# The output product by Strassen's form over pairs of token tiles, its weights' seven sides streamed from DRAM

## The chip, the cores and the metric

The kernel runs on one core of a Trainium2 chip. A core has TensorE (matrix products into PSUM), VectorE, ScalarE and GpSimd (elementwise work), and SyncE, whose queue issues most of the transfers here. The engines run their own instruction streams in order and wait for each other by semaphores. The time is device microseconds (us) of one execution; the times shown are the median of the runs and their range. Beside them stands one profiled execution, whose trace every view below comes from.

## The reference

Two stages in float32. The first is attention with root-mean-square norms on queries and keys: batch 8, 12 heads, 448 tokens, head size 64. The second is a gated feed-forward block on all 3584 tokens, model size 768, hidden size 1536. The weights come as float64.

```python
scores = scale * np.matmul(q_n, k_n.transpose(0, 1, 3, 2))
attn = softmax(scores)
x = np.matmul(attn, v).transpose(0, 2, 1, 3).reshape(B * S, H * D)
g = x @ w_gate
h = g * (1.0 / (1.0 + np.exp(-g))) * (x @ w_val)
out = h @ w_out
```

## The kernel before

**Stages.** The kernel proper is `fast`. Two batches make a block of 2 x 448 = 896 tokens; there are four blocks (NB). Attention for block 0 comes first. Then each block has an up phase (x by w_gate and w_val, giving the hidden rows `gt`, 128 partitions by 6 groups by 2 halves by 896 tokens, with the hidden features on the partitions) and a down phase (the hidden rows by w_out, giving the output rows). The attention of the next block, 12 head pairs, is woven into the down phase; the last block's down phase stands alone.

**The up phase** already uses a form of Strassen's algorithm (Winograd's, with seven products). `block(n)` (L946) calls `half_block(g, which)` (L955) for six groups and for gate and value. Each half block loads four quarters of the weight from the DRAM scratch `quarters` into a tile `ws` (L963, two buffers), and GpSimd makes three more sides out of them and changes a fourth (L969). TensorE does seven products of three matmuls each (L985), alternating between two PSUM banks, and VectorE adds the pieces up (L1001). The seven sides of x lie in `xs`; `sides` (L817, L833) makes the sums among them on VectorE, after the last head pairs of a block. SiLU is made of a tanh on ScalarE (L1035, L1088) and products on VectorE (L1040, L1095 for the gate; L1048, L1104 for the value, after which a group's hidden rows are done). The list `hidden` holds the last two of every group.

**The down phase before.** The 896 tokens are 7 tiles of 128. For each tile and each half of the 768 output columns, `out_rows` (L1116, L1120) multiplies 12 chunks of hidden features into one PSUM bank, in two parts of six matmuls. The weight `wo` lies in SBUF whole. The first part waits for groups 0 to 2 only, the second for 3 to 5. ScalarE copies the bank out (L1130) and issues the store (L1141), two transfers or one as the tile falls on the rows of the output.

**The weights.** They are float64. `convert` (L858) loads the raw words (SP), and ScalarE (L870, L874) and VectorE (L879, L882, L893, L897) make float32 of them. Twelve conversions make the quarters of w_gate and w_val, from staging places in `gt` and `wo` into a spare piece of `gt` or of `xs`, and from there they go to DRAM (L925). Six more make w_out, in place in `wo` (L934).

**The order of the work** is planned when the kernel is built. Every step is a piece of the class `Order`: an engine, an estimated duration, a due time `when`, what it comes after, and which buffers it takes. `run` (L417) sorts each engine's pieces by due time and takes, over and over, the piece that could start earliest by its model; a later piece is preferred to an earlier one if it could start more than 0.02 us sooner:

```python
                    if choice is None or at < choice[0] - 0.02:
                        choice = (at, piece)
```

The chosen order becomes the engines' instruction streams; on the chip each engine keeps to it and waits where its operands aren't there. `port=True` marks VectorE and GpSimd pieces that the planner never lets overlap. The due times of a block come from constants (L558), where UP, DOWN and BOTH are the planned lengths of an up phase, of a down phase alone and of one with attention:

```python
    UP, DOWN, BOTH = 14 * NG * PRODUCT, 111.0, 212.0
```

In attention (L584) the steps that the text speaks of are: the transposes of queries and keys on TensorE (L667), the scores (L705), the exponentials on ScalarE (L715), their sums on GpSimd (L721, L724), the weighted values on TensorE (L753), the reciprocal and the division on VectorE (L796, L806), and GpSimd's inverse root of the norm (L635) and its scaling (L647).

Of the kernel before, what the change touches and what calls it, by code (L numbers as in the profile page):

```python
# [9 lines left out]
F32 = mybir.dt.float32  # L10
# [3 lines left out]
ALU = mybir.AluOpType  # L14
# [346 lines left out]
class Order:  # L361
# [22 lines left out]
    def add(  # L384
        self, engine, us, when, emit, after=(), takes=(), uses=(), port=False, kb=0, group=None,
        mode=None, early=None,
    ):
        piece = dict(
            engine=engine, us=us, when=when, emit=emit, takes=takes, port=port, kb=kb,
            group=group, mode=mode, early=early,  # L390
            after=[a for a in after if a is not None], end=None, n=len(self.pieces),
        )
# [24 lines left out]
    def run(self, lookahead=400):  # L417
        left = {}
        for piece in sorted(self.pieces, key=lambda p: (p["when"], p["n"])):
            left.setdefault(piece["engine"], []).append(piece)  # L420
        while any(left.values()):
            best = None
            for engine, pieces in left.items():
                choice = None
                last = self.last.get(engine, dict(group=None))
                for piece in pieces[:lookahead]:
                    at = self.start(piece)
                    if at is None:
# [12 lines left out]
            at, piece = best  # L441
# [21 lines left out]
def fast(  # L463
# [30 lines left out]


    nc = tc.nc
    B, H, S, D = q.shape
# [12 lines left out]
    NK = NW // 2  # L510
    NG = NF // 2


# [43 lines left out]
    PRODUCT = 2.27  # L557
    UP, DOWN, BOTH = 14 * NG * PRODUCT, 111.0, 212.0  # L558

# [257 lines left out]
    def sides(n, c, when):  # L817
# [33 lines left out]
    flat_gt = gt.rearrange("p g f t -> p (g f t)")  # L851
    flat_wo = wo.rearrange("p f c -> p (f c)")
# [50 lines left out]
    def up_weights(i, when):  # L903
# [24 lines left out]

    def down_weights(f, when):

        rows = moe_w_out.rearrange("(f p) c -> p f c", p=P)[:, ts(f, 2), :]
        place = (5, 4, 5, 5, 2, 2)[f]
        weights["o", f] = convert(
            lambda raw: nc.sync.dma_start(raw.rearrange("p (f c) -> p f c", f=2), rows),  # L934
            flat_wo[:, ts(f, 2 * DM)],
            place, when, [staged.get(3 + f // 2)],
        )


# [6 lines left out]
    def block(n):  # L946
# [8 lines left out]
        def half_block(g, which):  # L955
# [159 lines left out]

        def out_rows(bank, i, half, part):  # L1116

            for g in range(part * NG // 2, (part + 1) * NG // 2):
                for f in range(2):
                    nc.tensor.matmul(  # L1120
                        banks[bank][:, 0:HALF],
                        gt[:, g, f, ts(i, P)],
                        wo[:, f * NG + g, ts(half, HALF)],
                        start=(g == 0 and f == 0),
                        stop=(g == NG - 1 and f == 1),
                    )

        def evacuate(bank, i, half):
            rows = take("rows", (n, i, half), [P, HALF])
            nc.scalar.copy(rows, banks[bank][:, 0:HALF])  # L1130

        def store(i, half):

            rows = tiles["rows", (n, i, half)]
            at = first = i * P
# [7 lines left out]

        groups = [(i, half) for i in range(2 * S // P) for half in range(2)]
        span = (BOTH if n < NB - 1 else DOWN) / (2 * len(groups))
        for k, (i, half) in enumerate(groups):
            bank = turn[0]
            turn[0] = 1 - bank
            for part in range(2):
                last = add(  # L1150
                    "PE", 3.93, start + UP + (2 * k + part) * span,
                    lambda bank=bank, i=i, half=half, part=part: out_rows(bank, i, half, part),
                    after=[*hidden[part * NG : (part + 1) * NG], last, bank_read[bank]]
                    + ([weights["o", f] for f in range(NG)] if n == 0 else []),
                    mode="full",
                )
            when = start + UP + (2 * k + 2) * span
            bank_read[bank] = add(
                "ACT", 0.48, when, lambda bank=bank, i=i, half=half: evacuate(bank, i, half),
                after=[last], takes=[("rows", (n, i, half))],  # L1160
            )
            add(
                "ACT", 0.15, when, lambda i=i, half=half: store(i, half),
                after=[bank_read[bank]], uses=[("rows", (n, i, half))], kb=192,
            )
        down_done[n] = last
# [18 lines left out]
    for i in range(2 * NG):  # L1185
        up_weights(i, 14.0 + 13.0 * i)
    for f in range(NF // 2):
        down_weights(f, 14.0 + 13.0 * 2 * NG + 14.0 * f)
    for m in range(EARLY):
# [73 lines left out]
```

## Time and profile before

| | |
|---|---|
| median of the runs (range) | 1667.47 us (1666.97 to 1668.51) |
| the profiled execution: its time, its span | 1668.56 us, 1666.7 us |
| TensorE busy, weight loads | 1625.9 us (98%), 808.4 us (49%) |
| VectorE, ScalarE, GpSimd busy | 670.6, 401.6, 681.9 us |
| first stretch: attention alone | 0 to 169.4 us |
| an up phase (block 1), the down phase after it | 566.7 to 761.5, 761.5 to 965.0 us |
| last block: up phase, down phase and tail | 1363.3 to 1552.7, 1552.7 to 1666.7 us |
| HBM read, written | 99.09 MB, 20.45 MB |

The span runs from the first to the last instruction that the trace holds; the execution's own time is somewhat longer. A group of instructions in the profile is one source line on one engine, with the tiles that it writes and reads. A float32 matmul leaves two records in it. Engines overlap, so busy times don't add up to the span; what counts is which engine ends each stretch and what it waited for. The phases overlap a little at their seams, since the planner draws attention's first pieces into the end of an up phase.

### The profile page before, as it was taken

The numbers are of one execution on the slowest core, as the hardware profiler recorded it, in microseconds if no ns is written. First come the engines' busy times: TensorE is split into PE (matmuls) and PEld (weight loads), VectorE is DVE, ScalarE is ACT, GpSimd is POOL, SyncE is SP. The second block draws the span as 40 slices with busy tenths as digits, with TensorE's granted clock in tenths as the row PEclk, the third lists the DMA queues.
The fourth block names the chain that finished last, engine by engine and source line by source line (L and its number), as shares of the span: only waits on it lengthen the run. The fifth ranks groups of instructions, "written<-read, shape, count | busy, mean of one in ns | idle before, by whom it ended". The sixth has DMA issues, their size and how long they took to land.

```text
span 1666.7 us, 14502 instructions
## 1 busy us (share of the span) xinstructions
PE 1625.9 (98%) x5616; PEld 808.4 (49%) x5616; DVE 670.6 (40%) x689; ACT 401.6 (24%) x537; POOL 681.9 (41%) x452
## 2 busy tenths in 40 slices
PE   5998999999999999999999999999999999999998
PEld 2333455545444455544545455554454545555555
DVE  5899763343334333333324333343323433333100
ACT  5765331123332110122333200102333211001000
POOL 5653223356675222445566502244567532221000
PEclk9999999999999999999999999999999999999999
DMA  8885531301111011221111111221211101111010
GB/s 234 250 235 184 183 146 64 96 28 48 54 43 67 11 57 57 66 71 44 48 48 42 58 42 39 68 76 37 64 48 49 63 15 57 38 57 39 15 29 25
DMA packets 73009, 120.57 MB, mean 72 GB/s; under 512 B 5860, under 2 KB 63716, under 8 KB 72932
## 3 DMA queue, kind: packets, MB, share of 16 engines
q1 hardware_dynamic: 63648, 108.54, 20.6%
q10 hardware_dynamic: 9284, 11.02, 2.3%
q8 instruction: 46, 0.75, 0.2%
q14 instruction: 31, 0.25, 0.0%
HBM read 99.09 MB, written 20.45 MB: 72 GB/s over the span
## 4 chain that ended last, share of the span: by engine, by line
PE 89%; DVE 4%; DMA 2%; issue 2%; POOL 1%; ACT 1%; SPq 0%; ACTq 0%; POOLq 0%; DVEq 0%
PE mm L985 46%; PE mm L1120 25%; PE at L753 9%; PE st L705 8%; PE st L667 2%; DVE xs L833 1%; DVE inv L796 1%; POOL t L647 1%; DMA qk<-in_q_dram 1%; POOL rr L635 1%; DMA wo<-in_moe_w_val_dram 1%; DMA gt<-in_moe_w_gate_dram 1%; DMA wo<-in_moe_w_gate_dram 0%; ACT e L715 0%; ACT gt L870 0%
## 5 line engine op out<-in xcount | busy, mean ns | idle before, releaser
L985 PE MATMUL mm<-xs,ws 128*128 128x448 f32 x2016 | 764.1, 541 | 5.2 <-DVE xs L833 5.2
L985 PEld LDWEIGHTS mm<-xs,ws 128*128 128x128 f32 x2016 | 382.8, 191 | 381.5 <-issue 371.5
L1120 PE MATMUL mm<-wo,gt 128*128 128x384 f32 x1344 | 449.9, 490 | 0.0
L969 POOL TENSOR_TENSOR ws<-ws 128x384 f32<-128x384 f32 x192 | 200.5, 1055 | 512.4 <-DMA ws<-quarters 433.0
L1120 PEld LDWEIGHTS mm<-wo,gt 128*128 128x128 f32 x1344 | 250.0, 190 | 191.1 <-issue 31.5
L635 POOL TENSOR_TENSOR rr<-ss,minus_half 112x16 f32<-112x16 f32 x48 | 143.7, 2993 | 243.0 <-DVE ss L627 208.3
L796 DVE RECIPROCAL inv<-at 128x448 f32<-128x448 f32 x48 | 141.9, 2956 | 190.2 <-PE at L753 190.1
L715 ACT ACTIVATE e<-st 112x896 f32<-112x896 f32 x192 | 165.7, 914 | 205.6 <-PE st L705 118.6
L705 PE MATMUL st<-QT,KT 64*112 64x448 f32 x768 | 172.0, 568 | 14.7 <-ACT e L715 6.9
L753 PE MATMUL at<-e,v 112*64 112x448 f32 x768 | 161.0, 545 | 0.0
L724 POOL TENSOR_TENSOR sums<-sums,e 112x896 f32<-112x896 f32 x72 | 151.4, 2102 | 18.8 <-ACT e L715 13.7
L1001 DVE TENSOR_TENSOR s<-s,mm 128x448 f32<-128x448 f32 x96 | 59.6, 621 | 155.4 <-PE mm L985 155.4
L705 PEld LDWEIGHTS st<-QT,KT 64*112 64x112 f32 x768 | 60.9, 174 | 116.8 <-issue 72.6
L647 POOL TENSOR_TENSOR t<-qk,rr 112x512 f32<-112x512 f32 x96 | 111.1, 1173 | 3.8
L721 POOL TENSOR_TENSOR sums<-e 112x896 f32<-112x896 f32 x36 | 75.7, 2102 | 69.2 <-PE at L753 66.2
L688 DVE TENSOR_SCALAR QT<-st,gg 128x448 f32<-128x448 f32 x37 | 25.3, 683 | 180.0 <-ACT KT L680 179.9
L1024 ACT COPY s<-mm 128x448 f32<-128x448 f32 x48 | 25.5, 532 | 294.6 <-PE mm L985 294.6
L1130 ACT COPY rows<-mm 128x384 f32<-128x384 f32 x56 | 26.9, 480 | 288.0 <-PE mm L1120 288.0
L753 PEld LDWEIGHTS at<-e,v 112*64 112x64 f32 x768 | 50.9, 136 | 88.7 <-issue 81.0
L1001 DVE TENSOR_TENSOR wide<-s,mm 128x448 f32<-128x448 f32 x72 | 44.7, 620 | 102.6 <-PE mm L985 102.6
L1001 DVE TENSOR_TENSOR gt<-s,mm 128x448 f32<-128x448 f32 x72 | 44.7, 621 | 99.1 <-PE mm L985 99.1
L1088 ACT ACTIVATE wide<-gt 128x1344 f32<-128x1344 f32 x24 | 31.8, 1323 | 178.0 <-DVE gt L1001 178.0
(58 smaller groups left out, 712.1 us busy)
## 6 DMA issues: line engine op xcount, KB each, us to landing
ws<-quarters SPq DMA_DIRECT2D x48, 768.0 KB, 4.3
qk<-in_q_dram SPq DMA_DIRECT2D x48, 224.0 KB, 3.4
qk<-in_k_dram SPq DMA_DIRECT2D x48, 224.0 KB, 3.6
v<-in_v_dram SPq DMA_DIRECT2D x48, 224.0 KB, 2.9
gt<-in_moe_w_gate_dram SPq DMA_DIRECT2D x8, 768.0 KB, 8.4
wo<-in_moe_w_val_dram SPq DMA_DIRECT2D x8, 768.0 KB, 8.4
wo<-in_moe_w_out_dram SPq DMA_DIRECT2D x4, 1536.0 KB, 7.6
quarters<-gt SPq DMA_DIRECT2D x7, 768.0 KB, 4.5
```

The source lines that it names most:

```text
L635: nc.gpsimd.tensor_tensor(out=rr.rearrange("p x h j one -> p (x h j one)"), in0=tiles["ss", m], in1=minus_half, op=ALU.pow,)
L647: nc.gpsimd.tensor_tensor(out=tiles["t", m][:, :, x].rearrange("p j h d -> p h j d"), in0=tiles["qk", (m, x)], in1=tiles["rr", m][:, x].to ...
L705: nc.tensor.matmul(st[0:R, h, 0:S], tiles["KT", m][rows, j, :], tiles["QT", m][rows].rearrange("p j r -> p (j r)"), start=True, stop=True,)
L715: nc.scalar.activation(e, tiles["st", (m, j)][0:R, :, 0:S], AF.Exp)
L721: nc.gpsimd.tensor_tensor(out=to, in0=tiles["e", (m, 0)], in1=e, op=ALU.add)
L724: nc.gpsimd.tensor_tensor(out=to, in0=to, in1=e, op=ALU.add)
L753: nc.tensor.matmul(to[ds(D * h, D), 0:S], lhs(h), rhs[:, h], start=first, stop=last)
L796: nc.vector.reciprocal(inv, tiles[den][:, 0:S])
L969: lambda to=to, a=a, b=b: nc.gpsimd.tensor_tensor(out=tiles[key][:, to], in0=tiles[key][:, a], in1=tiles[key][:, b], op=ALU.subtract,),
L985: nc.tensor.matmul(into[:, 0:S], w[:, side, c, :], xs[:, side, c], start=(fresh and c == 0), stop=(c == NK - 1), skip_group_check=not fina ...
L1001: nc.vector.tensor_tensor(out=to(), in0=one(), in1=two[:, 0:S], op=ALU.add)
L1120: nc.tensor.matmul(banks[bank][:, 0:HALF], gt[:, g, f, ts(i, P)], wo[:, f * NG + g, ts(half, HALF)], start=(g == 0 and f == 0), stop=(g == ...
```

## The change

The down phase takes the up phase's form of the algorithm. The 7 token tiles are three pairs and a single one. Of each pair and the two halves of the hidden features, A11 and A12 are the even tile's halves, A21 and A22 the odd tile's; the weight's quarters are its two halves of rows by its two halves of columns. Seven products of 6 matmuls of 128x384 give a pair's four output pieces; the single tile takes four products, with the weight's sides as they are for A11, A12, S1 and S4. The products go side by side: first A11 for all tiles, then A12, S2, A21, A22, S1 and S4.

- Sums of the hidden rows: VectorE makes S1 and S2 per group into a new tile `hs`, S3 in place of A21, and S4, in one instruction for all groups, in place of A12 once A12's products are through.
- The weight's seven sides are in DRAM (`out_sides`) instead of in SBUF; each is loaded (1152 KB) into the tile `ws` that the up phase uses, for its three or four products.
- `down_weights` converts a pair of row chunks into `hs`, GpSimd makes four more sides, and SP stores seven to DRAM. One pair comes after the other. Staging for the conversions moves from `wo` to a new tile `stage` and to `hs`; the spare targets are one in `gt` and one in `hs`, in turn.
- Evacuation: ScalarE copies only A11's products out; the others are added to a partial sum by VectorE, which leaves finished rows in `rows` (three buffers instead of two), and ScalarE issues the stores.
- The planner: pieces have a `rank` that is taken off their due time in the sorting (60 us for the up phase's VectorE pieces), a later piece must start more than 0.2 us sooner to be preferred, and DOWN and BOTH are 99 and 200.

The diff, cut to its core:

```diff
-        for piece in sorted(self.pieces, key=lambda p: (p["when"], p["n"])):
+        for piece in sorted(self.pieces, key=lambda p: (p["when"] - p["rank"], p["n"])):
...
-                    if choice is None or at < choice[0] - 0.02:
+                    if choice is None or at < choice[0] - 0.2:
...
-        qk=4, v=2, t=2, QT=2, KT=2, e=4, sums=1, inv=1, rows=2, st=2, at=2, ss=2, rr=2,
-        ws=2, s1=1, s2=1, s3=1, wide=1,
+        qk=4, v=2, t=2, QT=2, KT=2, e=4, sums=1, inv=1, rows=3, st=2, at=2, ss=2, rr=2,
+        ws=2, s1=1, s2=1, s3=1, wide=1, part=7,
...
-    wo = const.tile([P, NF, DM], F32, name="wo")
...
+    out_sides = [dram.tile([P, NG, HALF], F32, name=f"out_sides{i}") for i in range(7)]
...
+    hs = const.tile([P, 2, NG, NT // 2 * P], F32, name="hs")
+    stage = const.tile([P, 2 * 2 * DM], F32, name="stage")
...
-    UP, DOWN, BOTH = 14 * NG * PRODUCT, 111.0, 212.0
+    UP, DOWN, BOTH = 14 * NG * PRODUCT, 99.0, 200.0
...
-        if n == 0:
-            last.append(weights[spare[1]])
...
-    places = [flat_gt[:, ts(i, WORDS)] for i in range(3)] + [flat_wo[:, ts(i, WORDS)] for i in range(3)]
+    places = [flat_gt[:, ts(i, WORDS)] for i in range(3)] + [stage, flat_hs[:, 0:WORDS]]
...
-        if i % 2 or i > NG + 2:
-            dst, last = flat_gt[:, 3 * WORDS :], spare[0]
-            spare[0] = i
-        else:
-            dst, last = xs[:, S4 : S1 + 1].rearrange("p s c t -> p (s c t)"), spare[1]
-            spare[1] = i
+        dst, last = (flat_gt[:, 3 * WORDS :], flat_hs[:, WORDS:])[i % 2], spare[i % 2]
+        spare[i % 2] = i
         dst = dst[:, 0 : 4 * NK * P]
-        last = convert(src, dst, i % 6, when, [weights.get(last)])
+        last = convert(src, dst, i % 5, when, [weights.get(last)])
...
+    def down_weights(g, when):
+
+        rows = moe_w_out.rearrange("(two g p) c -> p g two c", p=P, two=2)[:, g]
+        to = flat_hs[:, 0 : 8 * HALF].rearrange("p (s c) -> p s c", s=8)
+
+        last = convert(
+            lambda raw: nc.sync.dma_start(raw.rearrange("p (two c) -> p two c", two=2), rows),
+            flat_hs[:, 0 : 4 * HALF],
+            (3, 2, 3, 3, 3, 3)[g], when,
+            [weights.get(i) for i in spare] + [staged.get(4), weights.get(("o", g - 1))],
+        )
+        for x, a, b in ((4, 1, 0), (5, 3, 4), (6, 3, 1), (7, 2, 5)):
+            last = order.add(
+                "POOL", 0.93, when,
...
+        def store():
+            for side, x in enumerate((0, 2, 6, 3, 4, 5, 7)):
+                nc.sync.dma_start(out_sides[side][:, g], to[:, x])
+
+        weights["o", g] = order.add("SP", 3.0, when, store, after=[last], kb=7 * 192)
...
-                return add("DVE", us, when + k * PRODUCT + 0.5, emit, after=after, **more)
+                return add(
+                    "DVE", us, when + k * PRODUCT + 0.5, emit, after=after, rank=60.0, **more
+                )
...
+            s = combine(sums(0, g), side(2, g), side(3, g), ALU.add, when, before)
+            summed["s1", g] = s
+            s = combine(sums(1, g), sums(0, g), side(0, g), ALU.subtract, when, [s])
+            summed["s2", g] = s
+            s = combine(side(2, g), side(0, g), side(2, g), ALU.subtract, when, [s])
+            summed["s3", g] = s
...
+        def multiply(bank, key, x, i):
+            w = tiles[key].rearrange("p s c f -> p (s c f)")[:, 0 : NG * HALF]
+            of = tokens(x, i)
+            for g in range(NG):
+                nc.tensor.matmul(
+                    banks[bank][:, 0:HALF],
+                    of(g),
+                    w[:, ts(g, HALF)],
+                    start=(g == 0),
+                    stop=(g == NG - 1),
+                )
...
+        products = [
+            (side_of, i)
+            for side_of in (A11, A12, S2, A21, A22, S1, S4)
+            for i in range(last_pairs + (side_of in (A11, A12, S1, S4)))
+        ]
+        span = (BOTH if n < NB - 1 else DOWN) / len(products)
...
+        for k, (x, i) in enumerate(products):
+            when = start + UP + k * span
+            key = ("ws", (n, "o", x))
+            if x not in loads:
+                loads[x] = add(
+                    "SP", 0.45, when - 24.0,
...
+                    after=[weights["o", g] for g in range(NG)], takes=[key], kb=1152, early=10.0,
+                )
...
+            if x == S4 and s4 is None:
+                s4 = combine(
+                    side(1), side(1), sums(1), ALU.subtract, when - 20.0,
+                    used12 + [summed["s2", g] for g in range(NG)],
+                )
...
+            last = add(
+                "PE", 3.93, when,
+                lambda bank=bank, key=key, x=x, i=i: multiply(bank, key, x, i),
+                after=[*hidden, *need, last, loads[x], bank_read[bank]], uses=[key], mode="full",
+            )
...
+                return add(
+                    "DVE", 0.56, when, emit, after=[m, made.get(one)],
+                    takes=[to] if takes else [], uses=[one] + ([] if takes else [to]),
+                )
...
+            if x == A11:
+                done = add(
+                    "ACT", 0.48, when,
...
+            elif x == A12:
+                done = finish_rows(one, 2 * i, 0)
+            elif x == S2 or (x == S1 and single):
+                done = made[one] = plus(one, one, False)
+            elif x == A21:
+                done = made[three] = plus(three, one, True)
+            elif x == A22:
+                done = finish_rows(three, 2 * i + 1, 0)
+            elif x == S1:
+                finish_rows(three, 2 * i + 1, 1)
+                done = made[one] = plus(one, one, False)
+            else:
+                done = finish_rows(one, 2 * i, 1)
+            bank_read[bank] = done
```

More of the change, by code (lines that the diff above doesn't have):

```diff
@@ L385, in add @@
         self, engine, us, when, emit, after=(), takes=(), uses=(), port=False, kb=0, group=None,
[L386 removed]
+        mode=None, early=None, rank=0.0,
     ):
@@ L1114, in block @@
         up_done[n] = last
[L1116 to L1134, printed above, removed]
+        def side(x, g=None):
+            f, tile_of = ((0, 0), (1, 0), (0, 1), (1, 1))[x]
+            pairs = gt[:, :, f, 0 : (NT - 1) * P].rearrange("p g (i two t) -> p g i two t", two=2, t=P)
+            pairs = pairs[:, :, :, tile_of]
+            return pairs if g is None else pairs[:, g]
@@ new lines, in sums, with combine @@
+        def sums(x, g=None):
+            pairs = hs[:, x].rearrange("p g (i t) -> p g i t", t=P)
+            return pairs if g is None else pairs[:, g]
+        def combine(to, one, two, op, when, after):
+            return add(
+                "DVE", 0.55, when,
+                lambda: nc.vector.tensor_tensor(out=to, in0=one, in1=two, op=op),
+                after=after, port=True,
+            )
+        summed = {}
+        for g in range(NG):
+            when = start + 14 * (g + 1) * PRODUCT + 6.0
+            before = [*hidden[2 * g : 2 * g + 2], down_done.get(n - 1)]
+            if n == 0:
+                before += [weights["o", x] for x in range(NG)]
+            s = combine(sums(0, g), side(2, g), side(3, g), ALU.add, when, before)
[4 more added lines that the diff above has]
+            summed["s3", g] = s
@@ L1135, in store @@
+        def store(key, i, half):
+            rows = tiles[key]
             at = first = i * P
@@ L1142, in store @@
                 at += size
-        groups = [(i, half) for i in range(2 * S // P) for half in range(2)]
-        span = (BOTH if n < NB - 1 else DOWN) / (2 * len(groups))
-        for k, (i, half) in enumerate(groups):
+        made = {}
+        last_pairs = NT // 2
+        products = [
[4 more added lines that the diff above has]
+        span = (BOTH if n < NB - 1 else DOWN) / len(products)
@@ L1147, in block @@
             bank = turn[0]
             turn[0] = 1 - bank
[L1149 to L1155, printed above, removed]
-                )
@@ L1157, in block @@
[L1157 to L1160, printed above, removed]
-            )
[L1162 to L1165, printed above, removed]
+            if x == S4 and s4 is None:
+                s4 = combine(
+                    side(1), side(1), sums(1), ALU.subtract, when - 20.0,
+                    used12 + [summed["s2", g] for g in range(NG)],
+                )
+                s4["us"] = 2.5
@@ new lines, in block, with plus, emit @@
+            if x == A12:
+                used12.append(last)
+            when += 3.93
+            single = i == last_pairs
+            def plus(to, one, takes, m=last, bank=bank, when=when):
+                def emit():
+                    dst = tiles[to] if to in tiles else take(*to, [P, HALF])
+                    nc.vector.tensor_tensor(
+                        out=dst, in0=tiles[one], in1=banks[bank][:, 0:HALF], op=ALU.add
+                    )
+                return add(
+                    "DVE", 0.56, when, emit, after=[m, made.get(one)],
+                    takes=[to] if takes else [], uses=[one] + ([] if takes else [to]),
+                )
@@ new lines, in block, with finish_rows @@
+            one, three = ("part", (n, i)), ("part", (n, i, 3))
+            def finish_rows(base, tile_of, half, when=when):
+                rows = ("rows", (n, tile_of, half))
+                done = plus(rows, base, True)
+                add(
+                    "ACT", 0.15, when + 0.6,
+                    lambda: store(rows, tile_of, half), after=[done], uses=[rows], kb=192,
+                )
+                return done
+            if x == A11:
+                done = add(
+                    "ACT", 0.48, when,
+                    lambda bank=bank, one=one: nc.scalar.copy(
+                        take(*one, [P, HALF]), banks[bank][:, 0:HALF]
+                    ),
+                    after=[last], takes=[one],
+                )
+                made[one] = done
+            elif x == A12:
[11 more added lines that the diff above has]
+                done = finish_rows(one, 2 * i, 1)
```

42 lines of the change are left out of this document (31 added, 11 removed).

## The prediction

> **What bounds the kernel now.** I read the head of the page first, then the stretches of the span cut at the changes of phase, then who waited for whom on TensorE, then the chain that ended last.
>
> ```profile
> span 1666.7 us, 14502 instructions
> PE 1625.9 (98%) x5616; PEld 808.4 (49%) x5616; DVE 670.6 (40%) x689; ACT 401.6 (24%) x537; POOL 681.9 (41%) x452
> ```
>
> ```profile
> 0.00:169.40 169.40, 134.96 (x683) 53.51 (x683) 140.08 (x112) 104.95 (x122) 84.71 (x52) 0.99 0.76 228
> ...
> 363.20:566.70 203.50, 203.26 (x833) 100.39 (x832) 77.00 (x66) 57.91 (x83) 122.31 (x68) 1.00 0.16 48
> 566.70:761.50 194.80, 194.80 (x538) 98.37 (x537) 68.02 (x91) 26.86 (x39) 60.79 (x52) 1.00 0.17 56
> ...
> 1552.70:1666.70 114.00, 108.39 (x337) 63.52 (x335) 2.18 (x2) 6.71 (x14) 0.00 (x0) 1.00 0.09 25
> ```
>
> The columns after each stretch's length are the busy microseconds of TensorE's matmuls (PE), its weight loads (PEld), VectorE (DVE), ScalarE (ACT) and GpSimd (POOL), the granted clock, the DMA share and GB/s. The first stretch is the attention that comes ahead of all blocks: TensorE idles 169.40 - 134.96 = 34.4 us there. From 169.4 us on it doesn't idle in an up phase (566.70:761.50), and 0.24 us in a down phase with the next attention woven in (363.20:566.70); the last down phase stands alone and ends in a tail without TensorE. The granted clock is 0.99 to 1.00. So from 169.4 us to the tail, the time is TensorE's instructions one behind another.
>
> ```profile
> PE st L667 <- POOL t L647: 11.0, 1, 11.0
> PE st L705 <- ACT e L715: 6.9, 11, 2.0
> PE st L705 <- ACT KT L680: 5.9, 1, 5.9
> PE mm L985 <- DVE xs L833: 5.2, 1, 5.2
> ```
>
> ```profile
> 1363.31 189.42 PE mm L985 x504
> 1552.73 108.37 PE mm L1120 x336
> ```
>
> The waits of TensorE (total, times, longest) all lie in the first stretch. The chain ends with the last block: 504 records of the up product, then 336 of the output product (L1120), and nothing else. A matmul leaves two records, so the 336 are 168 matmuls, and one costs 108.37 / 168 = 0.645 us.
>
> The profiled execution took 1668.56 us, 1.9 us more than its span; the three timed runs have a median of 1667.47 us, 1.1 us below it. I sum against 1668.56 and subtract 1.1 at the end. The three runs lie within 1.5 us, and 0.2% of the time, 3.3 us, is about the smallest change that can be told from none here.
>
> **What is removed on TensorE.** Before, a block's output product has 7 token tiles x 2 halves x 12 = 168 matmuls of 384 columns. After, three pairs of tiles take 7 products each and the seventh tile, alone, takes 4 (A11, A12, S1 and S4 run one index further): 25 products x 6 = 150 matmuls of the same shape. 18 fewer in each of four blocks are 72 x 0.645 = 46.4 us. The same from the group below is 449.9 / 672 = 0.669 us each, so 48.2 us; that mean holds what it costs TensorE to change over between attention and output product, and the number of attention pieces doesn't change. I take 46.4, and 48.2 as the other end.
>
> ```profile
> L1120 PE MATMUL mm<-wo,gt 128*128 128x384 f32 x1344 | 449.9, 490 | 0.0
> L969 POOL TENSOR_TENSOR ws<-ws 128x384 f32<-128x384 f32 x192 | 200.5, 1055 | 512.4 <-DMA ws<-quarters 433.0
> L635 POOL TENSOR_TENSOR rr<-ss,minus_half 112x16 f32<-112x16 f32 x48 | 143.7, 2993 | 243.0 <-DVE ss L627 208.3
> L796 DVE RECIPROCAL inv<-at 128x448 f32<-128x448 f32 x48 | 141.9, 2956 | 190.2 <-PE at L753 190.1
> L1001 DVE TENSOR_TENSOR s<-s,mm 128x448 f32<-128x448 f32 x96 | 59.6, 621 | 155.4 <-PE mm L985 155.4
> L1130 ACT COPY rows<-mm 128x384 f32<-128x384 f32 x56 | 26.9, 480 | 288.0 <-PE mm L1120 288.0
> ```
>
> **What is added on VectorE and taken from ScalarE.** 14 ScalarE copies a block (0.48 us) become 4. VectorE reads the other 21 products: 24 additions (S1 is used twice for each pair), like L1001 at 0.62 us for 448 columns, scaled to 384 about 0.55 us: 13 us a block, into a stretch where VectorE is busy 77 of 203.5 us. They hide under TensorE as long as a product (6 x 0.645 = 3.87 us) is longer than the addition, as there are two banks; uncovered, they'd be 13 us a block.
>
> **The sums of the hidden rows.** Per block 18 combinations of 128x384 and one of 128x2304 (S4), from SBUF to SBUF. The nearest row is the four side sums of x:
>
> ```profile
> 532.60 6.31 DVE L833 TENSOR_TENSOR xs<-xs 128x448 f32<-128x448 f32 x4
> ...
> 562.47 2.36 DVE L833 TENSOR_TENSOR xs<-xs 128x448 f32<-128x448 f32 x4
> ```
>
> ```profile
> 531.24 4.52 POOL L724 TENSOR_TENSOR sums<-sums,e 112x896 f32<-112x896 f32 x2
> 535.72 5.00 POOL L969 TENSOR_TENSOR ws<-ws 128x384 f32<-128x384 f32 x4
> ```
>
> Beside GpSimd one takes 6.31 / 4 = 1.58 us, without it 0.59. For 384 columns: 0.51 to 1.35 us, so 9 to 24 us a block; I take 14, as most fall where GpSimd is busy 60.79 of 194.8 us. They lie in the up phase (VectorE 68.0 of 194.8 us). Only the last group's three come after it, and their reader S2 stands behind 8 products (31 us). S4's takes 3.0 (0.59 x 2304 / 448) to 8.1 us, and stands beside S1's four products (15.5 us). So: nothing on the path.
>
> [...]
>
> **The weights' sides and the queues they pass.** In each down phase SP issues 7 loads of 1152 KB into the two buffers of ws, in a queue that carried only q, k and v there.
>
> ```profile
> ws<-quarters SPq DMA_DIRECT2D x48, 768.0 KB, 4.3
> ...
> wo<-in_moe_w_out_dram SPq DMA_DIRECT2D x4, 1536.0 KB, 7.6
> ```
>
> Between 4.3 us for 768 KB and 7.6 for 1536 KB lies about 6 us. A load can start when the side before last is through, so it has at least three products: 11.6 us alone, twice that with attention between. SP waits in order, so a load behind a q, k or v load that waits for its buffer comes as late as that wait overruns its plan; the slack is 5 us in the last block, where no such loads are left, and over 15 us in the others. The next block's first quarter now waits for S1's end; behind it stand four products (15.5 us) against 4.3 us of load and two subtractions of 1.06 us. Nothing on the path.
>
> Before block 0's down phase, the six row pairs of w_out are converted through one region: ScalarE, four VectorE steps, four GpSimd subtractions, seven stores, then the next pair.
>
> ```profile
> 173.73 0.96 DVE L879 TENSOR_SCALAR wo<-wo 128x1536 f32<-128x1536 f32 x1 [1.81 <-ACT wo L870]
> ...
> 181.19 1.75 DVE L897 CUSTOM_DVE_ANT_0 wo<-wo 128x3072 uint16<-128x3072 uint16 x1
> ```
>
> ```profile
> L870 ACT ACTIVATE wo<-wo 128x1536 f32<-128x1536 f32 x4 | 6.5, 1630 | 24.7 <-DMA wo<-in_moe_w_out_dram 24.7
> ```
>
> ```profile
> 220.14 7.38 POOL L969 TENSOR_TENSOR ws<-ws 128x384 f32<-128x384 f32 x4 [11.34 <-DMA ws<-quarters]
> ```
>
> One link: 1.6 us on ScalarE, 9.2 on VectorE with the up phase's work between (173.73 to 182.94), 4.2 (four times 1.055) to 7.4 on GpSimd, 7 to 8 for 1344 KB of stores, by the loads above: 22 to 26 us. Six from 173 us end by 329 us, and the first side must leave 6 us or more ahead of the down phase (363 us), so by 355. Hidden, with 26 us to spare.
>
> **The seams.** The first product after the up phase now reads all six groups, where a part of three did; in the last block the end of the last group is here:
>
> ```profile
> 1552.77 0.62 DVE L1001 TENSOR_TENSOR wide<-s,mm 128x448 f32<-128x448 f32 x1 [1.63 <-PE mm L985]
> 1553.42 1.56 DVE L1104 SCALAR_TENSOR_TENSOR gt<-gt,wide 128x1344 f32<-128x1344 f32 x1
> ```
>
> It ends at 1554.98, and the sixth matmul comes 5 x 0.645 = 3.2 us after 1552.73, at 1555.9: covered. If the first matmul waited instead, 2.3 us a block. The tail is ScalarE's copy (0.48 us) and its store; after, VectorE adds (0.55 us) and ScalarE is told: +0.2 us.
>
> **The start.** Less certain: the tie width of the planner (0.02 to 0.2), the rank of the up phase's vector work and the staging reorder the first 169 us, where VectorE is busy 140.
>
> ```profile
> 162.74 1.76 DVE L897 CUSTOM_DVE_ANT_0 gt<-wo,gt 128x3072 uint16<-128x3072 uint16 x1
> 164.42 2.95 DVE L796 RECIPROCAL inv<-at 128x448 f32<-128x448 f32 x1
> ```
>
> ```profile
> ACT gt L870 <- DMA quarters<-gt: 3.1, 1, 3.1
> ```
>
> Block 0 waits 5.2 us for its side sums, behind a reciprocal that stood behind the last conversion, which had to share its target with the one before; now targets alternate. Bounds: the 5.2 us go, or as much again comes from the new order. I take -1.
>
> Sum: 1668.56 - 46.4 + 0.2 - 1.0 = 1621.4 us; less 1.1, **1620.3 us**.
>
> **The rivals.**
> Part of it is lost in waits (0.12): with less output product to fill in, TensorE meets attention's latency in blocks 0 to 2. The gain there is 34.8 us; a quarter of it gone gives about 1629 us. For it: VectorE has some 30 us of new work a block (13 + 14 + 3). Against it: 0.24 us of waiting in 203.5 now, and VectorE and GpSimd at 77 and 122 us.
>
> w_out's sides come late (0.06): from 22 to 26 us a link it would take (355 - 173) / 6 = 30.3 us a link before block 0's first side is late; at 34 us, the load is 6 x 3.7 = 22 us late, so about 1642 us. For it: the chain is serial. Against it: the 26 us to spare.
>
> Slower (0.05): ScalarE's store of a row tile now waits for an addition on VectorE, which may stand behind a reciprocal and its product (2.96 + 0.62 us); the exponentials behind that store come late, and TensorE, with two score buffers, stops. There are 14 stores in each of three such phases. From (46.4 + 3.3) / 42 = 1.2 us of TensorE's time for each store it decides; at 2 us, 84 us, so about 1704 us. Against it: VectorE idles 126 of 203.5 us, and another bank lets TensorE go on.
>
> No change (0.03): TensorE's busy share, whose ends are modelled, says nothing, and something else sets the pace; then about 1667 us. The head of the page shows weight loads at 49%. [...] The trace speaks against it: 168 matmuls followed one another at 0.645 us in the last 108 us while VectorE and GpSimd did 2.2 us of work.
>
> That the count doesn't fall is not open: it follows from the loops.
>
> **How the numbers follow.** Forecast 0.74, rivals 0.12, 0.06, 0.05 and 0.03. The forecast's own range is 1620.3 less 1.8 (48.2 us) less 4.2 (the 5.2 us gone): 1614; and plus 6 (5 more at the start instead of -1) plus 2.3 (one seam): 1629. Taking in the first rival and a little past it, 1612 to 1634 holds 0.74 + 0.12 less the tails. Faster 0.92, same 0.03, slower 0.05.
>
> **What would show it.** Right: 1200 records of the output product, 0.645 us a matmul in the last block, its down phase 96.8 us instead of 108.4; the interleaved phases shorter by 11 to 12 us each with under 1 us of waiting; block 0 starting between 164 and 175 us. Wrong: waits of TensorE on VectorE's additions or on ws in the down phases, a gap ahead of block 0's first side, exponentials behind a store, or a matmul of another price.

## The result

The changed kernel takes 1629.07 us (median of four runs, 1627.47 to 1629.51), the kernel before 1667.29 us (four runs; the 1667.47 us above is the median of three). The ratio is 0.977, with a 95% interval of 0.975 to 0.979. That is 38.2 us less, where 47.2 us less was forecast. The profiled execution took 1629.46 us, its span is 1627.5 us.

The head of the page, and the span cut at its phases (columns as before: busy TensorE, its weight loads, VectorE, ScalarE, GpSimd, clock, DMA share, GB/s):

```profile
span 1627.5 us, 14620 instructions
PE 1582.9 (97%) x5472; PEld 781.3 (48%) x5472; DVE 770.2 (47%) x861; ACT 382.8 (24%) x497; POOL 702.8 (43%) x476
```

```profile
172.00:240.00 68.00, 68.00 (x183) 34.36 (x182) 38.94 (x44) 15.84 (x15) 27.08 (x27) 1.00 0.45 154
240.00:311.41 71.41, 66.15 (x188) 33.76 (x186) 46.34 (x48) 16.53 (x20) 43.22 (x35) 1.00 0.52 172
...
761.80:948.60 186.80, 186.80 (x771) 91.96 (x770) 85.34 (x86) 52.13 (x72) 113.42 (x62) 1.00 0.25 79
948.60:1149.00 200.40, 200.40 (x565) 99.89 (x564) 83.42 (x113) 27.90 (x40) 69.30 (x58) 1.00 0.22 71
...
1525.20:1627.50 102.30, 96.77 (x301) 56.67 (x299) 19.26 (x30) 1.91 (x4) 0.00 (x0) 0.99 0.29 97
```

TensorE doesn't idle in a down phase with attention (761.80:948.60) nor in the up phase behind it. It idles 71.41 - 66.15 = 5.26 us between 240 and 311 us, in block 0's up phase, where it had no wait before. The waits of TensorE on its products name the two places; the first of the three rows is the start of block 0, which had 5.2 us before:

```profile
PE mm L1001 <- DVE xs L838: 6.0, 1, 6.0
...
PE mm L1001 <- DVE s L1019: 3.5, 1, 3.5
PE mm L1001 <- ACT s L1042: 1.8, 1, 1.8
```

The chain that ended last, at the starts of blocks 1 to 3 and at the end:

```profile
561.45 171.38 PE mm L1001 x456
...
948.58 171.47 PE mm L1001 x456
...
1335.80 189.42 PE mm L1001 x504
1525.22 96.76 PE mm L1182 x300
```

Set beside the chain of before (block starts at 169.40, 566.71, 965.01 and 1363.31 us, end of TensorE at 1661.1), the 39.2 us of span fall out like this. Block 0 starts at 168.78 us, 0.6 us earlier. From there to block 1 it takes 392.67 us instead of 397.31, so 4.6 less. Block 1 takes 387.13 us instead of 398.30, 11.2 less, block 2 11.1 less, the last block 11.6 less, and the tail 0.1 less. Forecast were 18 x 0.645 = 11.6 us a block; blocks 1 to 3 gave that to about half a microsecond each. Block 0 gave 6.5 us less than its neighbours.

The groups of the new work, and the new loads:

```profile
L1182 PE MATMUL mm<-ws,gt 128*128 128x384 f32 x912 | 308.3, 491 | 0.0
L1182 PE MATMUL mm<-ws,hs 128*128 128x384 f32 x288 | 97.0, 490 | 0.0
L1254 DVE TENSOR_TENSOR rows<-part,mm 128x384 f32<-128x384 f32 x56 | 31.0, 553 | 146.4 <-PE mm L1182 130.7
```

```profile
ws<-out_sides SPq DMA_DIRECT2D x28, 1152.0 KB, 5.2
```

### The profile page after: what moved, and what is told of

Its sections match the earlier page's. It is cut to its first block, busy times and chain, and to the rows that moved or that the text cites. A ratio compares the mean times of both kernels' runs of the same rounds, so it can differ in the third digit from the quotient of the medians.

```text
span 1627.5 us, 14620 instructions
## 1 busy us (share of the span) xinstructions
PE 1582.9 (97%) x5472; PEld 781.3 (48%) x5472; DVE 770.2 (47%) x861; ACT 382.8 (24%) x497; POOL 702.8 (43%) x476
## 4 chain that ended last, share of the span: by engine, by line
PE 81%; DVE 0%; issue 0%
PE mm L1001 38%; PE mm L1182 24%; PE at L760 9%; PE st L712 7%; PE st L674 2%; DVE hs L1150 0%; DVE rows L1254 0%; DVE s L1019 0%; DVE gt L1150 0%
## 5 line engine op out<-in xcount | busy, mean ns | idle before, releaser
L1001 PE MATMUL mm<-xs,ws 128*128 128x448 f32 x2016 | 765.2, 541 | 11.3 <-DVE xs L838 6.0
L1001 PEld LDWEIGHTS mm<-xs,ws 128*128 128x128 f32 x2016 | 383.0, 191 | 389.2 <-issue 373.5
L985 POOL TENSOR_TENSOR ws<-ws 128x384 f32<-128x384 f32 x192 | 194.2, 1021 | 445.7 <-DMA ws<-quarters 298.6
L1182 PE MATMUL mm<-ws,gt 128*128 128x384 f32 x912 | 308.3, 491 | 0.0
L1182 PEld LDWEIGHTS mm<-ws,gt 128*128 128x128 f32 x912 | 168.9, 190 | 136.8 <-issue 30.6
L722 ACT ACTIVATE e<-st 112x896 f32<-112x896 f32 x192 | 165.8, 914 | 279.9 <-PE st L712 187.9
L1019 DVE TENSOR_TENSOR s<-s,mm 128x448 f32<-128x448 f32 x96 | 59.5, 620 | 110.4 <-PE mm L1001 108.3
L1042 ACT COPY s<-mm 128x448 f32<-128x448 f32 x48 | 25.6, 532 | 318.2 <-PE mm L1001 318.2
L1254 DVE TENSOR_TENSOR rows<-part,mm 128x384 f32<-128x384 f32 x56 | 31.0, 553 | 146.4 <-PE mm L1182 130.7
L1182 PE MATMUL mm<-ws,hs 128*128 128x384 f32 x288 | 97.0, 490 | 0.0
L1019 DVE TENSOR_TENSOR gt<-s,mm 128x448 f32<-128x448 f32 x72 | 44.7, 621 | 105.2 <-PE mm L1001 105.1
L1019 DVE TENSOR_TENSOR wide<-s,mm 128x448 f32<-128x448 f32 x72 | 44.7, 620 | 103.8 <-PE mm L1001 103.8
```

What stands on the lines that cost most here:

```text
L722: nc.scalar.activation(e, tiles["st", (m, j)][0:R, :, 0:S], AF.Exp)
L985: lambda to=to, a=a, b=b: nc.gpsimd.tensor_tensor(out=tiles[key][:, to], in0=tiles[key][:, a], in1=tiles[key][:, b], op=ALU.subtract,),
L1001: nc.tensor.matmul(into[:, 0:S], w[:, side, c, :], xs[:, side, c], start=(fresh and c == 0), stop=(c == NK - 1), skip_group_check=not fina ...
L1019: nc.vector.tensor_tensor(out=to(), in0=one(), in1=two[:, 0:S], op=ALU.add)
L1182: nc.tensor.matmul(banks[bank][:, 0:HALF], of(g), w[:, ts(g, HALF)], start=(g == 0), stop=(g == NG - 1),)
```

## The experiments

The theory: the 6.5 us are in block 0's up phase, where w_out's conversions and the sums of the hidden rows stand in the in-order queues of VectorE and ScalarE ahead of instructions that free a PSUM bank. The two places in the trace are these. On VectorE, six sums stand in one heap ahead of the addition L1019:

```profile
302.50 0.62 DVE L1058 SCALAR_TENSOR_TENSOR gt<-gt,mm 128x448 f32<-128x448 f32 x1 [2.14 <-ACT gt L1053]
303.04 1.22 DVE L1150 TENSOR_TENSOR hs<-gt 128x384 f32<-128x384 f32 x1
304.36 2.18 DVE L1150 TENSOR_TENSOR hs<-hs,gt 128x384 f32<-128x384 f32 x1
306.46 1.36 DVE L1150 TENSOR_TENSOR gt<-gt 128x384 f32<-128x384 f32 x1
307.74 1.34 DVE L1150 TENSOR_TENSOR hs<-gt 128x384 f32<-128x384 f32 x1
309.18 1.18 DVE L1150 TENSOR_TENSOR hs<-hs,gt 128x384 f32<-128x384 f32 x1
310.28 0.55 DVE L1150 TENSOR_TENSOR gt<-gt 128x384 f32<-128x384 f32 x1
310.75 0.61 DVE L1019 TENSOR_TENSOR s<-s,mm 128x448 f32<-128x448 f32 x1
```

In block 0 the sums wait for all six pairs of w_out, since these are converted in the same tile `hs`; the last pair is stored by about 301 us, so two groups' sums came at once. On ScalarE, a conversion step that waits for raw words from DRAM stands ahead of the copy out of PSUM:

```profile
250.00 1.55 ACT L879 ACTIVATE stage<-stage 128x1536 uint32<-128x1536 uint32 x1 [2.27 <-DMA stage<-in_moe_w_out_dram]
251.45 0.51 ACT L1042 COPY s<-mm 128x448 f32<-128x448 f32 x1
```

The rivals: contention (the sums, 1.18 to 2.18 us each beside GpSimd and 0.55 us without it, and the DMA traffic cost what they cost wherever they stand), the planner's new settings, and TensorE's own order (two pairs' transposes stood between two products there).

**Spreading the sums** (`e1_spread`).

```diff
             when = start + 14 * (g + 1) * PRODUCT + 6.0
+            early = None
+            if n == 0:
+                when, early = start + UP - 45.0 + 9.0 * g, 0.0
```

> The changed kernel with block 0's sums of the hidden rows held back by the planner and spread, three every 9 us, over the end of the up phase. Theory (queue): the sums stood in one heap in VectorE's in-order queue in front of an addition that frees a PSUM bank, TensorE waited 3.5 us for it and lost about 1.9 us more to a lowered clock; spread, both are gone, so about 5 us less, near 1624 us, while the 1.8 us wait behind ScalarE stays. Rival (contention): the sums, slowed by GpSimd, and the DMA traffic take TensorE's time wherever they stand; then 1629 us. Rival (planner): the wider tie width does it; then 1629 us too.

Measured: 1623.36 us (1622.32 to 1623.53). The sums now alternate with the additions, and of TensorE's waits in block 0 one on ScalarE is left:

```profile
302.56 1.20 DVE L1150 TENSOR_TENSOR hs<-gt 128x384 f32<-128x384 f32 x1
303.71 0.62 DVE L1019 TENSOR_TENSOR s<-s,mm 128x448 f32<-128x448 f32 x1
304.25 0.83 DVE L1150 TENSOR_TENSOR hs<-hs,gt 128x384 f32<-128x384 f32 x1
```

```profile
PE mm L1001 <- ACT s L1042: 1.7, 1, 1.7
```

The gain, 5.7 us, is more than the wait of 3.5 us. About 2 us more are the clock: behind the wait of the changed kernel (first row) it was granted at 0.60, in the same stretch of the spread kernel (second row) at 1.00. Two smaller terms nearly cancel: in the profiled execution block 0 starts 1.1 us earlier (167.69 against 168.78 us), and its first 212 records take 0.7 us longer (82.19 against 81.45).

```profile
312.00:316.00 4.00, 4.00 (x8) 1.99 (x7) 2.07 (x5) 0.00 (x0) 0.00 (x0) 0.60 0.00 0
```

```profile
312.00:316.00 4.00, 4.00 (x12) 1.99 (x11) 2.65 (x3) 0.98 (x2) 0.99 (x1) 1.00 0.87 299
```

**Leaving the heap out** (`e10_no_heap`). The spread also moved the transposes, so this one keeps every order.

```diff
-                lambda: nc.vector.tensor_tensor(out=to, in0=one, in1=two, op=op),
+                lambda: None if skip else nc.vector.tensor_tensor(out=to, in0=one, in1=two, op=op),
...
-            s = combine(sums(0, g), side(2, g), side(3, g), ALU.add, when, before)
+            s = combine(sums(0, g), side(2, g), side(3, g), ALU.add, when, before, n == 0 and g < 2)
```

> The changed kernel with every engine's order kept, but block 0's first six sums of the hidden rows (groups 0 and 1) left out, the ones that stand ahead of the addition that TensorE waited 3.5 us for. Theory (queue): the wait goes and the clock isn't lowered behind it, 1623 to 1624 us. Rival (TensorE's own order): the planner put two pairs' transposes between two products there, and the spread moved them too; if they are the cause, the wait stays and the time is 1628 to 1629 us.

Measured: 1624.05 us (1622.44 to 1625.47). The addition starts 1.68 us behind its predecessor's start instead of 8.25, the 3.5 us wait is gone, and the transposes are where they were. Together with the spread, in which every sum is still made, that shows the heap's place in the queue as the cause, and TensorE's order not.

```profile
303.68 0.62 DVE L1058 SCALAR_TENSOR_TENSOR gt<-gt,mm 128x448 f32<-128x448 f32 x1 [2.14 <-ACT gt L1053]
305.36 0.62 DVE L1019 TENSOR_TENSOR s<-s,mm 128x448 f32<-128x448 f32 x1 [1.06 <-PE mm L1001]
```

**The planner's price** (`e2_price`).

```diff
-                "DVE", 0.55, when,
+                "DVE", 1.3 if n == 0 else 0.55, when,
```

> The changed kernel with one number changed: the planner counts 1.3 us instead of 0.55 us for each of block 0's sums of the hidden rows, about what they take beside GpSimd. Theory (queue): the planner then lets the additions of the up phase in between, the 3.5 us wait goes and with it the lowered clock, near 1624 us. Rival (contention): 1629 us. If only the heap's place moves and it waits elsewhere, 1626 to 1629 us.

Measured: 1628.36 us (1628.25 to 1629.73). A miss: with the dearer price the planner put the same six sums ahead of the same addition, and the wait of 3.5 us stayed. The price alone doesn't break the heap. A likely reason, not shown by a run, is that by the planner's clock nothing else was ready.

```profile
310.85 0.55 DVE L1150 TENSOR_TENSOR gt<-gt 128x384 f32<-128x384 f32 x1
311.32 0.61 DVE L1019 TENSOR_TENSOR s<-s,mm 128x448 f32<-128x448 f32 x1
```

**The planner's settings.** First taken out of the changed kernel (`e4_oldplan`), then put alone into the kernel before (`e5_plan_alone`).

```diff
-                    if choice is None or at < choice[0] - 0.2:
+                    if choice is None or at < choice[0] - 0.02:
...
-                    "DVE", us, when + k * PRODUCT + 0.5, emit, after=after, rank=60.0, **more
+                    "DVE", us, when + k * PRODUCT + 0.5, emit, after=after, rank=0.0, **more
```

> The changed kernel with the planner's settings of before: tie width 0.02 and rank 0. Rival (planner): the settings cost block 0 its 6.5 us, about 1622.5 us. Theory (queue): the settings are not the cause; the waits in the first 310 us come out elsewhere, 1626 to 1632 us, and the phases of blocks 1 and 2 are as long as in the changed kernel (387.2 us) or up to 2 us longer.

> The kernel before, with the change's planner settings alone (tie width 0.2, rank 60 for the up phase's VectorE pieces), no Strassen in the output product. They are worth about 12 us inside the changed kernel, whose block 0 is crowded on VectorE. Theory (queue): before the change block 0 showed no wait of TensorE but one of 5.2 us, so there is nothing for them to save: 1664 to 1671 us. Rival (planner): part of the change's gain is theirs by themselves; then 1655 to 1662 us.

Measured: 1641.26 us (1639.62 to 1642.22) without them in the changed kernel, 12.2 us more, which is outside what both expected; and 1668.42 us alone, a ratio of 1.0008 (0.9999 to 1.0017) to the kernel before. So they are worth nothing in the kernel before and 12 us in the changed one. That the fuller VectorE queue of block 0 makes the difference fits the waits below but was argued, and the two settings (tie width and rank) were not tried one by one. Without them TensorE has these waits on VectorE in the products, all in block 0's up phase but the third, while blocks 1 and 2 take 387.13 us each, as in the changed kernel (387.13 and 387.22):

```profile
PE mm L1001 <- DVE gt L1058: 6.2, 2, 3.8
...
PE mm L1001 <- DVE s L1019: 3.7, 2, 2.2
PE mm L1001 <- DVE xs L838: 3.3, 1, 3.3
PE mm L1001 <- DVE gt L1066: 3.3, 1, 3.3
```

**ScalarE's wait and the start.** Five kernels tried to take them away.

Where an experiment adds lines to the kernel, the line numbers behind them move by one to three: L1059 and L1060 below are the L1058 of the changed kernel, L1020 its L1019, L1043 its L1042, L1055 its L1053, L1003 its L1001, L1185 its L1182.

`e3_stage` gave the third and fifth pairs of w_out another staging place:

```diff
-            (3, 2, 3, 3, 3, 3)[g], when,
+            (3, 2, 5, 3, 5, 3)[g], when,
```

> The changed kernel with a second staging place for the conversions of w_out (rows of the hidden tile that block 0 writes last), so that the raw words of the fifth pair are on their way one conversion earlier. Theory (queue): ScalarE's conversion, in front of a PSUM copy in its queue, no longer waits for its transfer, the 1.8 us wait of TensorE goes, about 1627 us; the 3.5 us wait stays unless the order around it happens to change. Rival (contention): the DMA queues are as full, no change, 1629 us.

Measured: 1632.02 us (1630.72 to 1633.85). In this kernel the third pair's raw words (load issued at 184.58 us) land on a part of the second's before that is converted (its last step starts at 200.91 us), so those words of the second pair are lost. The 1.7 us wait stayed, and one of 2.3 us on VectorE (L1059) came on top. A miss.

`e9_spread_stage` moved the fourth pair instead, behind the second, with the sums spread:

```diff
-            (3, 2, 3, 3, 3, 3)[g], when,
+            (3, 2, 3, 5, 3, 3)[g], when,
...
+        if g == 3:
+            staged[5] = staged[2]
```

> The spread sums of the first experiment, and the fourth pair of w_out staged in rows of the hidden tile that block 0 writes last, after the second pair has left the rows under them, so that the raw words of pairs four and five come one conversion earlier. Theory (queue): ScalarE's step that waits for raw words no longer does so ahead of a PSUM copy; the 1.7 us wait goes without a longer chain: 1621.6 us. If another wait of block 0's up phase takes its place, as when the steps were put in turn, 1622.5 to 1624 us.

Measured: 1639.35 us (1638.62 to 1642.42), far off both. It shows the mechanism at its largest. The planner put the fourth pair's first ScalarE step ahead of block 0's tanh (L1055). The load of its raw words was issued at 203.99 us, and the step started 7.65 us later, about what such loads take (median 7.4 us into `stage`, 8.1 us into `gt` in this run); the releaser that its row names is inferred. So the step sat at the head of ScalarE's queue with 8.8 us idle before it; the tanh, VectorE's product behind it and TensorE followed. Another such wait cost 6.7 us later. The last number of the VectorE row is its idle time, 8.42 us; the row of TensorE ends with its wait of 5.32 us.

```profile
211.64 1.56 ACT L879 ACTIVATE gt<-gt 128x1536 uint32<-128x1536 uint32 x1 [8.82 <-DMA out_sides<-hs]
213.10 0.53 ACT L1055 ACTIVATE gt<-mm 128x448 f32<-128x448 f32 x1
```

```profile
213.66 0.62 DVE L1060 SCALAR_TENSOR_TENSOR gt<-gt,mm 128x448 f32<-128x448 f32 x1 [8.42 <-ACT gt L1055]
```

```profile
214.34 33.53 PE L1003 MATMUL mm<-xs,ws 128*128 128x448 f32 x84 [5.32 <-DVE gt L1060]
```

`e6_in_turn` has the sums spread and the two ScalarE steps in turn:

```diff
-            after=[loaded],
+            after=[loaded] + [one] * in_turn,
```

> The spread sums of the first experiment, and each conversion of w_out has its two ScalarE steps in turn, so that the one that waits only for the raw words no longer stands in the queue ahead of a PSUM copy. Theory (queue): the 1.7 us wait behind ScalarE's copy goes, about 1.7 us less than the first experiment's 1623.4 us, so 1621.7 us; the chain of conversions gets some 9 us longer, which nothing waits for. Rival (contention): the wait moves to another copy or to ws, 1623 us or more.

Measured: 1622.51 us (1622.29 to 1624.51). The wait behind ScalarE's copy went, and one of 1.0 us on VectorE (L1059), behind a later conversion, came. 0.9 us less than the spread alone is inside the runs' spread.

`e7_late` adds to that a later date for the last up conversion, `e11_all` adds the same to the kernel of `e9_spread_stage`:

```diff
-        up_weights(i, 14.0 + 13.0 * i)
+        up_weights(i, 14.0 + 13.0 * i + 8.0 * (i == 11))
```

> The experiment before (sums spread, conversions in turn), and the last conversion of the up weights is due 8 us later, behind the last reciprocal of block 0's attention instead of ahead of it on VectorE. Theory (queue): TensorE's wait of 5.4 us for the side sums of x shrinks by the 2 us that the reciprocal stood behind the conversion, and the lowered clock behind it shortens with it, so 1618.5 to 1620 us. Rival: the wait is the latency of reciprocal, division and sums, not the queue; then 1621.7 us as without it.

> The spread sums, the fourth pair's staging and the last up conversion due 8 us later, all three. Theory (queue): the three waits of block 0 are separate and their gains add: about 1.7 for ScalarE and 1.7 for the start, so 1620 us. If the planner pays for one with another, as it did when the last two were first tried, 1622 to 1625 us.

Measured: 1624.63 us (1622.61 to 1627.26) and 1623.16 us (1619.90 to 1623.87). In both the wait for x's side sums shrank as expected, from 5.4 and 5.2 to 3.3 us, so the reciprocal had stood behind the conversion. In the first, five waits of together 2.8 us came instead along block 0's up phase (behind ScalarE's copy L1043 and its exponentials L722, and VectorE's L1059 and L1020). In the second, 1.3 us on GpSimd's sides of ws came, and the two long waits of `e9_spread_stage` went, with one due time changed elsewhere. No combination is told apart from the spread alone; all four lie between 1622.5 and 1624.6 us, and beat both kernels.

**A price for TensorE** (`e8_five_groups`), on the kernel with the sums spread.

```diff
-            for g in range(NG):
+            for g in range(NG - 1):
```

> The first experiment's kernel with the sixth group of hidden features left out of every product of the down phase: 100 of 600 matmuls less, everything else kept. If TensorE's instructions one behind another set the time, 100 x 0.645 = 64.5 us less than 1623.4, so 1559 us. If VectorE's additions or the sides' loads are close behind TensorE, the gain is smaller: a product then takes 3.2 us, three of them 9.7 us against some 6 us of load; then 1565 us or more, with waits on ws or on the additions in the last block.

Measured: 1560.86 us (1558.97 to 1561.57), 62.5 us less for 100 matmuls, 2 us short of the 64.5; in the profiled execution block 0 starts 1.7 us later than with the spread alone (169.37 against 167.69 us). The last down phase:

```profile
1473.30 80.64 PE mm L1185 x250
```

80.64 / 125 = 0.645 us, the old price at a product a sixth shorter, without a wait in the down phases: neither VectorE's additions nor the sides' loads hold TensorE there even with products a sixth shorter.

## Why the prediction was right, and where it was off

**The count and the price of the matmuls** held: 912 + 288 = 1200 records instead of 1344, and 96.76 / 150 = 0.645 us. The last block gave 11.6 us. Blocks 1 and 2 gave 11.2 and 11.1. By TensorE's order in block 1, three more of the weighted sums now follow directly on transposes, which then take 0.86 us to the next start instead of 0.77; that is 0.3 of the 0.44 us, and the rest was not traced.

**VectorE's additions, the sides' loads, the seams and the tail** held: 0.55 us each as estimated, 5.2 us a load instead of some 6, no gap at 1525.22, and 5.5 us of tail, where 5.6 + 0.2 were forecast. **The start** gave 0.6 of the 1.0 us, but not by the wait that was to shrink: that rose from 5.2 to 6.0 us, and the reciprocal still starts right behind the last conversion's last step (162.12 and 163.79 us).

**What failed** is "nothing on the path" for the sums of the hidden rows and "hidden, with 26 us to spare" for w_out's conversions. Both were judged by when their last reader needs them and by how long VectorE idles in all. That part was right: the sums took (15.7 + 15.6 + 14.8) / 4 = 11.5 us a block, inside the 9 to 24, S4 took 2.6, and the last side was stored by about 301 us, earlier than the 305 to 329 forecast. But what cost time is who stood behind them in an in-order queue. The prediction also took the sums to come group by group; in block 0 they are held until w_out's sides are stored, and that made the heap. A wait for raw words on ScalarE held a PSUM copy, 1.8 us, and a heap of sums on VectorE held an addition, 3.5 us. The sum: 5.3 us of waits and 2 us of lowered clock, less about 0.8 us of clock that block 0 loses less at its start (before 0.55 for 5 us from 170 us on, after 0.64 for 4 us from 169 on), make 6.5 us.

**That the time lies in the range** is in part luck. The forecast's own upper end, 1629 us, was made of 6 us at the start and a seam; neither came, and the 6.5 us came from terms that the sum put at nothing.

**Of the rivals,** "part of it is lost in waits" gave 1629 us, which is the measured time, but by another mechanism: it placed the loss in the phases with attention, where TensorE waits for nothing. The rival of w_out's sides had the right work in the wrong role: the sides came in time, and their conversions cost time by standing in the queues. The slower rival and the no-change rival are refuted by the same rows, and the last by `e8_five_groups` too. **The planner's settings** were given the start alone, within 5 us; they are worth 12 us inside this change, in block 0.

Open: what decides that the planner's order for block 0 comes out well in one version and 16 us worse in another that differs by one due time (`e11_all` against `e9_spread_stage`). That is the order's sensitivity, seen but not traced.

## What to carry to other kernels

Work that is "hidden" is hidden for two readers: the one that needs its result, and the instruction behind it in its engine's queue. Check the second first, above all for steps that wait for DRAM or that become ready all at once. Where TensorE set the time here, its removed instructions came back nearly one for one (11.1 to 11.6 of 11.6 us in each of blocks 1 to 3), and what is lost is found by comparing the phases' lengths block by block.

## What the runs showed of the hardware

Behind a wait of 3.48 us the clock was granted at 0.60 (312 to 316 us), behind one of 1.79 us at 1.00 (253 to 257 us). After the first, 19 records took 9.10 us; at the pace of the up phase (189.42 us for 504) they'd take 7.14, so 2 us were lost behind a wait of 3.5. The row behind the second, the first one here, runs at about that pace, 54.39 us for 144 records where it gives 54.12:

```profile
252.01 54.39 PE L1001 MATMUL mm<-xs,ws 128*128 128x448 f32 x144 [1.79 <-ACT s L1042]
306.24 1.70 PE L674 MATMUL st<-ident,t 112*128 112x112 f32 x16
311.41 9.10 PE L1001 MATMUL mm<-xs,ws 128*128 128x448 f32 x19 [3.48 <-DVE s L1019]
```

Behind some shorter waits time was lost too. In `e4_oldplan` the 48 records behind a wait of 2.35 us took 20.00 us, where that pace gives 18.04, and the 36 behind a wait of 2.18 us took 13.80, where it gives 13.53 (mean granted clock from 169 to 300 us: 0.95). In `e3_stage`, the last row here (its L1002 is the L1001 of the changed kernel), the 114 behind a wait of 2.27 us took 44.80, where it gives 42.85 (mean clock in the same stretch: 0.97).

```profile
242.05 20.00 PE L1001 MATMUL mm<-xs,ws 128*128 128x448 f32 x48 [2.35 <-DVE gt L1058]
264.24 13.80 PE L1001 MATMUL mm<-xs,ws 128*128 128x448 f32 x36 [2.18 <-DVE s L1019]
```

```profile
210.33 44.80 PE L1002 MATMUL mm<-xs,ws 128*128 128x448 f32 x114 [2.27 <-DVE gt L1059]
```

So behind waits of 2.27, 2.35 and 3.48 us about 2 us more were lost each, behind one of 2.18 us 0.3 us. Whether the length alone decides, these few waits can't tell.

The sums of 384 columns took 0.55 us alone and 1.18 to 2.18 us in the heap, while GpSimd ran these:

```profile
302.81 2.36 POOL L654 TENSOR_TENSOR t<-qk,rr 112x512 f32<-112x512 f32 x2
305.13 4.81 POOL L985 TENSOR_TENSOR ws<-ws 128x384 f32<-128x384 f32 x4
```

GpSimd's instructions end at 303.85, 305.17, 306.12, 307.41, 308.68 and 309.94 us. Each of the first five sums ends 0.40 to 0.42 us after one of these ends, and the one of 2.18 us stood through two; the sixth began after the last of them and took 0.55 us. The heap took more than twice as long as six sums alone: 7.7 us from its first sum to the addition, where six of 0.55 us are 3.3. The 4.4 us between are more than the wait of 3.5 us, so by this estimate it took both to make the wait, the heap's place in the queue and the longer sums beside GpSimd. No run took GpSimd away.
